# Turning two query blocks by DMA instead of on TensorE at the head of an attention and feed-forward kernel

## The chip, the cores and the metric

The kernel runs on one core of one Trainium2 chip. The core has a matrix engine (TensorE, PE in the profile, with its weight loads as PEld), a vector engine (VectorE, DVE), a scalar engine (ScalarE, ACT), a general engine (GpSimd, POOL) and a queue engine (SyncE, SP) that issues most transfers. Sixteen DMA engines move the data. Each engine works through its own list of instructions in order; semaphores make one wait for another. The metric is the device time of one execution in microseconds (us), as the median of the runs.

## The reference

Two blocks follow each other. The first is attention without softmax: for each batch and head, `kv = k^T v` and `out = q kv`, then an RMS norm over the 64 elements of a head. The second is a multiplicative feed-forward network over the 4608 tokens so made.

```python
kv = np.einsum('bhsd,bhse->bhde', k, v)
out = np.einsum('bhsd,bhde->bhse', q, kv)
rms = np.sqrt(np.mean(out * out, axis=-1, keepdims=True) + 1e-06)
x = (out / rms * g_norm)            # then (B,H,S,D) -> (B*S, H*D)
h = (x @ w1) * (x @ w2) @ w3
return h @ w_out
```

There are 8 batches, 8 heads, 576 tokens and a head size of 64; the model size is 512 and the inner size 1024. `q`, `k` and `v` are 32-bit floats; the weights arrive as 64-bit floats.

## The kernel before, in words

**Overall order.** Since nothing stands between the product with `w3` and the one with `w_out`, the kernel first multiplies `w3` by `w_out` (the fold). Then it walks over nine groups of 512 tokens: one for each batch, and one for the 64 tokens that each batch has left over. For each group it makes the two gate products with `w1` and `w2`, multiplies them, and projects with the folded matrix. The products use Winograd's scheme of seven block products instead of eight, so sums of blocks are made on VectorE. The attention of the next group runs in pieces between the products of the present one.

**Weights.** A 64-bit weight tile is read as raw words into one of four `raw` buffers and made into 32-bit floats by `conversion` (L137): two passes on ScalarE (L165, L167), then four on VectorE: the top bits of the low part (L169), a clamp (L173), a shift (L176) and an addition (L181). `w1` and `w2` are also scaled by the norm's gain (L135 or L133). `conversion` is a generator: each `yield` is a point at which the caller may place other work. With `in_parts`, which only one weight tile has, there is one more such point. `load_next` (L200, transfers at L207) fills the next raw buffer.

**The fold.** It goes over the inner size in eight chunks, twice (the first half of `w3`'s rows, then the second). For each chunk `w3` must be turned: `turn_w3` does it on TensorE (L701) and ScalarE copies the result out (L703); for chunks 3, 5 and 7 of the second half `w3_by_dma` does it by a DMA transpose. `fold_chunk` (L717) then adds a chunk to four sums; after the last chunk ScalarE copies each sum out (L723). `keep_warm` (L287) puts products of no use on TensorE.

**A turn by DMA** (`turn_by_dma`, L289). The DMA transpose works on 16-bit words. So the lower and upper halves of the 32-bit words are first split into two planes (L308 or L306), the transpose is issued on SyncE (L310), and the planes are put together again (L320). The split and the copy back are on GpSimd, ScalarE or VectorE, as the caller says. It too is a generator, with a point between each of its steps.

**The first batch.** Its attention runs inside the second half of the fold, in the loop that begins at L1470. `begin_q` (L1472) turns two of the four query blocks on TensorE (`q_t`, L361, transposes at L367, copy out at L369) and then loads the next blocks into the buffers that come free (`load_q_ahead`, L94): blocks 0 and 1 before chunk 1, blocks 2 and 3 before chunk 4. `begin_kv` makes `kv` (L347, copies at L355 and L357). `product` (L411) makes `q kv` for half of the heads (L425) after chunks 2 and 5, and `norm` follows: squares on ScalarE (L392), a reduction on VectorE (L393), the root on ScalarE (L397), the reciprocal (L399) and the multiplication (L402) on VectorE. The half of the first product is turned by DMA (`x_first`, L1474), the other half on TensorE (`turn`, L461, copy at L463). `sum_w` (L828, L829) and `combine_x` (L818) make the first sums of blocks for the gates. A `qT` tile holds a turned query block; there are two such buffers.

**The first gates.** `winograd` runs seven products (L748). After the first, ScalarE copies the result away (L766) before the third product may reuse its bank.

**What sets the order.** In the fold every engine's list is written out by hand, in the order in which the source runs. After it TensorE, GpSimd and SyncE keep that order, and a scheduler places the work of VectorE and ScalarE, except where `issue_after` ties a step behind a named instruction. One of those ties, at L1622, begins the conversion of a weight tile in the first gates. It is tied to `copies["xT"]`, the last copy of the turned second half:

```python
ahead = [copies["p5"][p] if p else copies["xT"], copies["u3" if p == 1 else "u2"][p]][n]
with tc.issue_after(ahead.ins):
```

Of the kernel before, what the change touches and what calls it, by code (L numbers as in the profile page):

```python
# [22 lines left out]
def kernel(  # L23
# [32 lines left out]
    nc = tc.nc  # L56
# [80 lines left out]
    def conversion(  # L137
        n, dst, raw, cols=slice(0, 1024), scale=None, by_scalar=False, in_parts=False
    ):

        dst, raw = (t if len(t.shape) == 3 else t[:, cols] for t in (dst, raw))
        if raw.dtype == FP32:
            yield
            yield
            if in_parts:
                yield
            nc.vector.tensor_copy(out=dst, in_=raw)
            if scale is not None:
                scale_by(dst, scale, by_scalar)
            return  # L150
        words = raw.bitcast(U32).rearrange("p (n w) -> p n w", w=2)
        lo, hi = words[:, :, 0], words[:, :, 1]

        low = ab[n % 2][:, NF // 2:].rearrange("p a i t -> p (a i t)")[:, cols]
        low_bits = low.bitcast(U32)

        low_top = low.bitcast(U16).rearrange("p (n w) -> p n w", w=2)[:, :, 1]
        hi_top = raw.bitcast(U16).rearrange("p (n w) -> p n w", w=4)[:, :, 3]
        if len(dst.shape) == 3:
            wide = dict(c=dst.shape[1])  # L160
            lo, hi, low, low_bits = (
                t.rearrange("p (c n) -> p c n", **wide) for t in (lo, hi, low, low_bits)
            )
        dst_bits = dst.bitcast(U32)
        nc.scalar.activation(low, lo, AF.Copy, scale=2.0 ** -51, bias=2.0)  # L165
        yield
        nc.scalar.activation(dst, hi.bitcast(FP32), AF.Abs)  # L167
        yield
        nc.vector.tensor_scalar(  # L169
            out=low_top, in0=hi_top, scalar1=0x8000, scalar2=0x4000,  # L170
            op0=ALU.bitwise_and, op1=ALU.bitwise_or,
        )
        nc.vector.tensor_scalar(  # L173
            out=dst, in0=dst, scalar1=LEAST, scalar2=MOST, op0=ALU.max, op1=ALU.min
        )
        nc.vector.tensor_scalar(  # L176
            out=dst_bits, in0=dst_bits, scalar1=3, scalar2=None, op0=ALU.logical_shift_left
        )
        if in_parts:
            yield  # L180
        nc.vector.tensor_tensor(out=dst_bits, in0=dst_bits, in1=low_bits, op=ALU.add)  # L181
        yield
        if scale is not None:
            scale_by(dst, scale, by_scalar)
# [145 lines left out]
    def attention(b):  # L330
# [37 lines left out]
            qT[r] = work.tile([P, 2, 2, P], FP32, name="qT")  # L368
            nc.scalar.copy(qT[r], qt_ps)  # L369

        def q_by_dma(r, copy=None):

            qT[r] = work.tile([P, 2, 2, P], FP32, name="qT")
            q_sb = loaded["q", b, r].rearrange("p e n -> p (e n)")
            to = qT[r].rearrange("p e i t -> p (e i t)")
            return turn_by_dma([q_sb], to, q_sb, [to], copy or q_copy)

        st = {}

# [333 lines left out]
    def fold_chunk(half, c, ms, cols=slice(0, DM)):  # L713
        if c == 0 and 0 in ms and cols.start == 0:
            sums_ps[half] = [bank(ps_mm, "mm") for m in range(NH)]
        for m in ms:
            nc.tensor.matmul(  # L717
                sums_ps[half][m][:, cols], lhsT=w3T[half, c][:, m, :], rhs=chunks[:, c, 1, cols],
                start=(c == 0 and cols.start == 0), stop=(c == KF - 1),
                skip_group_check=(half == 0),  # L720
            )
            if c == KF - 1:
                nc.scalar.copy(w3o_sb[:, half * NH + m, :], sums_ps[half][m])  # L723


    late = {}
# [688 lines left out]
    with tc.manual_schedule(  # L1415
# [22 lines left out]
        for c in range(KF):  # L1438
# [11 lines left out]
            if c == 0:  # L1450
                for n in range(2):
                    fold_chunk(0, c, range(NH), slice(n * N, (n + 1) * N))
                begin_next(lambda: turn_w3(0, 1))
                keep_warm(2)
                continue
            fold_chunk(0, c, range(NH - 1))
            if c < 3:
# [11 lines left out]
        turns, SPLIT = {}, {0: 3, 2: 5, 4: 7}  # L1469
        for c in range(KF):  # L1470
            if c in BEGIN:
                first.begin_q(2 * BEGIN[c], 2 * BEGIN[c] + 1)  # L1472
                if c == max(BEGIN):
                    x_first = first.x_by_dma(0, nc.vector.tensor_copy, split=nc.scalar.copy)  # L1474
                    next(x_first)
# [4 lines left out]
            if c < KF - 2:  # L1480
                if c < max(BEGIN):
                    begin_next()
                if c == max(BEGIN) + 1:
                    for steps_of_w in begun[len(converted)]:
                        next(steps_of_w)
                    all_of(x_first)
                else:
                    end_next(False)
# [3 lines left out]
                    next(t)  # L1492
                if len(raws) < FIRST:
                    load_next()
                if c == 2:
                    for steps_of_w in begun[len(converted)]:
                        next(steps_of_w)
                elif c == max(BEGIN):
                    run(sum_w(0))
            elif c == KF - 2:  # L1500
                end_next(False)
# [12 lines left out]
            fold_chunk(1, c, range(1, NH - 1))  # L1514
            if c == 2:
                all_of(turns[c + 1])
            elif c + 1 < KF and c + 1 not in turns:
                turn_w3(1, c + 1)
            if c in (max(BEGIN), KF - 2):
# [2 lines left out]
            if c in PRODUCT:  # L1522
                norms[c] = first.product(PRODUCT[c])
                next(norms[c])
                if c > max(BEGIN):
                    all_of(turns[c + 2])
                next(norms[c])
    fold_cm.__exit__(None, None, None)
    late_pool = ctx.enter_context(tc.tile_pool(name="late", bufs=1, reuse_waits="tile"))
# [6 lines left out]
    for n, T in enumerate(groups):  # L1536
# [44 lines left out]
        for p in range(NF):  # L1581
# [22 lines left out]
            if T == 0:  # L1604
# [14 lines left out]
                        run(ops)  # L1619
                for n in range(2):  # L1620
                    if len(converted) < len(todo):
                        ahead = [copies["p5"][p] if p else copies["xT"], copies["u3" if p == 1 else "u2"][p]][n]  # L1622
                        with tc.issue_after(ahead.ins):
                            if p or n:
                                begin_next()
# [83 lines left out]
```

## Time and profile before

| what | value |
|---|---|
| median of 3 runs | 741.33 us (739.96 to 741.8) |
| the profiled execution's own time | 740.67 us |
| its span, first to last instruction | 738.8 us |
| granted clock of TensorE, mean | 1.0 |
| TensorE busy | 733.8 us, 99% of the span |
| VectorE busy | 629.1 us, 85% |
| ScalarE busy | 378.9 us, 51% |
| GpSimd busy | 22.2 us, 3% |
| the second half of the fold | about 44.7 to 79.3 us |

Times in the profile are counted from the first instruction. A timeline line has start, duration, engine, source line, operation, tiles (out <- in), shapes, how many records were merged, and in brackets how long the engine was idle before and what released it. Two records of TensorE stand for one matmul in 32-bit floats. A line of the waits has the waiting engine and line, what it waited for, the total, the number of times and the longest. In the chain of waits each line is a piece of the chain of work that ended last: start, duration, what.

### The profile page before, as it was taken

Reading aid. Unit: us, or ns where it says so; the run is one execution under the profiler, and the core shown is the slowest. Engines: PE = TensorE matmul, PEld = TensorE weight load, DVE = VectorE, ACT = ScalarE, POOL = GpSimd, SP = SyncE. Lnnn points to the kernel's source line nnn. Section 1 sums busy time; section 2 is a strip of 40 time slices with the busy share of each in tenths; the row PEclk is TensorE's granted clock in tenths of the full one; section 3 lists DMA queues with packets and bytes.
Section 4 is the critical chain, followed back from the end, with each engine's and each line's share of the span. In section 5 each row is a group of like instructions: output and inputs, shape, how many; then the busy total and the mean of one; then the engine's idle time right before and its main releaser. Section 6 shows DMA issues by size and latency. Waiting matters only on the chain.

```text
span 738.8 us, 16924 instructions
## 1 busy us (share of the span) xinstructions
PE 733.8 (99%) x6867; PEld 659.5 (89%) x6867; DVE 629.1 (85%) x1259; ACT 378.9 (51%) x660; POOL 22.2 (3%) x29
## 2 busy tenths in 40 slices
PE   8999999999999999999999999999999999999998
PEld 7445788888899999999999999999999999999998
DVE  7988898968879689968996899689969987997797
ACT  7787778415552675257626762576177313212321
POOL 0000000221000000000000001000001000000000
PEclk9999999999999999999999999999999999999999
DMA  9999925599989698869887988698847762565454
GB/s 318 351 331 244 288 94 144 148 337 300 334 254 317 177 279 258 261 173 289 249 269 168 294 248 268 170 294 234 264 102 222 227 208 86 180 216 161 133 197 142
DMA packets 138769, 170.44 MB, mean 231 GB/s; under 512 B 81220, under 2 KB 114116, under 8 KB 138692
## 3 DMA queue, kind: packets, MB, share of 16 engines
q1 hardware_dynamic: 136240, 155.02, 70.8%
q10 hardware_dynamic: 2452, 14.35, 5.8%
q8 instruction: 54, 0.88, 0.5%
q14 instruction: 23, 0.19, 0.1%
HBM read 130.55 MB, written 20.71 MB: 205 GB/s over the span
## 4 chain that ended last, share of the span: by engine, by line
PE 94%; DMA 2%; ACT 2%; DVE 1%; SPq 1%; issue 0%; ACTq 0%
PE mm L748 37%; PE mm L1298 23%; PE mm L1040 21%; PE mm L717 5%; PE at L347 2%; DMA raw<-in_moe_w_dram 2%; PE at L748 2%; PE mm L425 1%; PE at L425 1%; PE at L701 1%; PE at L1341 0%; ACT ab L165 0%; SPq L207 0%; PE at L444 0%; ACT xT L306 0%
## 5 line engine op out<-in xcount | busy, mean ns | idle before, releaser
L1089 ACT COPY slots<-mm 128x512 f32<-128x512 f32 x88 | 51.6, 587 | 127.0 <-PE mm L1298 83.6
L748 PE MATMUL mm<-xT,w_sb 128*128 128x256 f32 x448 | 102.9, 380 | 0.0
L748 PEld LDWEIGHTS mm<-xT,w_sb 128*128 128x128 f32 x448 | 84.6, 191 | 11.3 <-issue 0.5
L748 PE MATMUL mm<-xc,ws 128*128 128x256 f32 x336 | 76.4, 380 | 0.3 <-ACT inner_sums L766 0.3
L748 PEld LDWEIGHTS mm<-xc,ws 128*128 128x128 f32 x336 | 63.9, 190 | 9.1 <-ACT inner_sums L766 0.7
L766 ACT COPY slots<-mm 128x512 f32<-128x512 f32 x59 | 34.6, 586 | 70.0 <-PE mm L748 65.0
L717 PE MATMUL mm<-chunks,ab 128*128 128x512 f32 (+1 forms) x136 | 59.7, 578 | 0.5 <-DVE chunks L181 0.5
L1093 DVE TENSOR_TENSOR slots<-mm,slots 128x512 f32<-128x512 f32 x66 | 45.2, 684 | 17.1 <-PE mm L1040 17.0
L1090 ACT COPY slots<-mm 128x384 f32<-128x384 f32 x88 | 42.3, 481 | 26.3 <-PE mm L1298 23.8
L1040 PE MATMUL mm<-ws,w3o_sb 128*128 128x128 f32 x350 | 54.0, 275 | 0.0
L1298 PE MATMUL mm<-w3o_sb,ab 128*128 128x128 f32 x368 | 48.9, 276 | 0.0
L393 DVE TENSOR_REDUCE inv<-sq 128x8 f32<-128x512 f32 (+1 forms) x40 | 24.6, 630 | 27.6 <-ACT sq L392 27.5
L1040 PEld LDWEIGHTS mm<-ws,w3o_sb 128*128 128x128 f32 x350 | 46.4, 192 | 0.0
L1298 PEld LDWEIGHTS mm<-w3o_sb,ab 128*128 128x128 f32 x368 | 45.4, 192 | 0.6
L717 PEld LDWEIGHTS mm<-chunks,ab 128*128 128x128 f32 x136 | 23.6, 190 | 22.6 <-issue 15.5
L1298 PE MATMUL mm<-w3o_sb,raw 128*128 128x128 f32 x340 | 43.5, 275 | 0.0
L1298 PEld LDWEIGHTS mm<-w3o_sb,raw 128*128 128x128 f32 x340 | 40.7, 192 | 0.0
L748 PE MATMUL mm<-xc,w_sb 128*128 128x256 f32 x160 | 38.5, 384 | 0.0
L1094 DVE TENSOR_TENSOR slots<-mm,slots 128x384 f32<-128x384 f32 x66 | 36.4, 552 | 2.2 <-PE mm L1298 1.6
L748 PE MATMUL mm<-xT,ws 128*128 128x256 f32 x160 | 38.2, 382 | 0.0
L748 PEld LDWEIGHTS mm<-xT,ws 128*128 128x128 f32 x160 | 30.1, 190 | 4.2 <-ACT slots L766 0.2
L748 PEld LDWEIGHTS mm<-xc,w_sb 128*128 128x128 f32 x160 | 29.9, 190 | 4.2
(246 smaller groups left out, 1648.9 us busy)
## 6 DMA issues: line engine op xcount, KB each, us to landing
w3o_sb<-w_l SPq DMA_DIRECT2D x21, 896.0 KB, 6.0
w3o_sb<-w3o_l SPq DMA_DIRECT2D x18, 896.0 KB, 6.4
raw<-in_moe_w_dram SPq DMA_DIRECT2D x31, 512.0 KB, 7.7
raw<-w3o_l SPq DMA_DIRECT2D x15, 896.0 KB, 4.7
w3o_sb<-w3o_l ACTq DMA_DIRECT2D x14, 896.0 KB, 4.6
k_sb<-in_k_dram SPq DMA_DIRECT2D x16, 576.0 KB, 5.0
v_sb<-in_v_dram SPq DMA_DIRECT2D x16, 576.0 KB, 5.9
q_sb<-in_q_dram SPq DMA_DIRECT2D x32, 256.0 KB, 4.8
```

The lines of the kernel that those rows point to most:

```text
L347: nc.tensor.matmul(ps[r * D:(r + 1) * D, :], lhsT=k_sb[rows, r, cols], rhs=v_sb[rows, r, cols], start=(j == 0), stop=(j == JS - 1),)
L393: adds["norm"] = nc.vector.tensor_reduce(out=inv[:, i], in_=sq.rearrange("p (h d) -> p h d", d=D), axis=AX.X, op=ALU.add)
L425: nc.tensor.matmul(o_ps[l][tokens, n * D:(n + 1) * D], lhsT=qT[r][rows, e, i, tokens], rhs=kv_b[rows, m // 2 ^ l, e, h, :], start=True, st ...
L717: nc.tensor.matmul(sums_ps[half][m][:, cols], lhsT=w3T[half, c][:, m, :], rhs=chunks[:, c, 1, cols], start=(c == 0 and cols.start == 0), s ...
L748: nc.tensor.matmul(ps[:, u, :], lhsT=lhsT(a_name, u, c), rhs=rhs(b_name, c),  start=(u == 0 and c == 0 and new), stop=(c == chunks - 1), s ...
L766: copies.setdefault(name, []).append(nc.scalar.copy(t, ps))
L1040: nc.tensor.matmul(ps[place // 4][:, place % 4, :], lhsT=x, rhs=y, start=new and place // 4 not in seen, stop=True, skip_group_check=True,)
L1089: nc.scalar.copy(z[:, 0:4], ps[0])
L1090: return nc.scalar.copy(z[:, 4:7], ps[1][:, 0:3])
L1093: nc.vector.tensor_add(z[:, 0:4], ps[0], z[:, 0:4])
L1094: nc.vector.tensor_add(z[:, 4:7], ps[1][:, 0:3], z[:, 4:7])
L1298: nc.tensor.matmul(ps[place // 4][:, place % 4, :], lhsT=x[:, c, :], rhs=y[:, c, :], start=new and place // 4 not in seen, stop=(c == 1), ...
```

## The change

Six edits, all before the end of the first gates:

- The third and fourth query block of the first batch (2 and 3) are turned by DMA transposes and no longer by `begin_q` on TensorE. Block 2 is split on ScalarE and block 3 on VectorE, after chunk 2's turn and ahead of the first norm; the two transposes are issued at chunk 3; at chunk 4 VectorE copies both back, ahead of `sum_w`.
- With that the loads of the next query blocks move on SyncE behind the transposes of `x_first` and of chunk 7.
- In the weight tile with `in_parts` there are now points after the first VectorE pass and after the clamp. The clamp runs between the second norm's reduction and its reciprocal, the shift and the addition behind the norm; before, clamp and shift ran ahead of the copies back of `x_first`.
- The extra point for weights that are already 32-bit floats goes; no tile of this case takes that branch.
- Four small products of no use are added before the second chunk of the fold.
- The first conversion of the gates is tied behind the last copy of the fold instead of the last `xT` copy.

```diff
 (conversion, 64-bit branch)
         nc.vector.tensor_scalar(out=low_top, in0=hi_top, ...)
+        if in_parts:
+            yield
         nc.vector.tensor_scalar(out=dst, in0=dst, scalar1=LEAST, scalar2=MOST, ...)
+        if in_parts:
+            yield
         nc.vector.tensor_scalar(out=dst_bits, in0=dst_bits, scalar1=3, ...)
-        if in_parts:
-            yield
         nc.vector.tensor_tensor(out=dst_bits, in0=dst_bits, in1=low_bits, op=ALU.add)
...
-        def q_by_dma(r, copy=None):
+        def q_by_dma(r, copy=None, split=None):
...
-            return turn_by_dma([q_sb], to, q_sb, [to], copy or q_copy)
+            return turn_by_dma([q_sb], to, q_sb, [to], copy or q_copy, split)
...
-                nc.scalar.copy(w3o_sb[:, half * NH + m, :], sums_ps[half][m])
+                copies["w3o"] = nc.scalar.copy(w3o_sb[:, half * NH + m, :], sums_ps[half][m])
...
                 begin_next(lambda: turn_w3(0, 1))
-                keep_warm(2)
+                keep_warm(2, 4)
...
             if c in BEGIN:
-                first.begin_q(2 * BEGIN[c], 2 * BEGIN[c] + 1)
+                if c == min(BEGIN):
+                    first.begin_q(0, 1)
...
                 if c == max(BEGIN) + 1:
-                    for steps_of_w in begun[len(converted)]:
-                        next(steps_of_w)
+                    steps_of_w, = begun[len(converted)]
+                    next(steps_of_w, None)
                     all_of(x_first)
...
+                if c == 3:
+                    for t in q_turns:
+                        next(t)
...
                 elif c == max(BEGIN):
+                    for r, t in enumerate(q_turns):
+                        all_of(t)
+                        first.load_q_ahead(2 + r)
                     run(sum_w(0))
...
             if c == 2:
                 all_of(turns[c + 1])
+                q_turns = [
+                    first.q_by_dma(2 + r, nc.vector.tensor_copy, split)
+                    for r, split in enumerate((nc.scalar.copy, nc.vector.tensor_copy))
+                ]
+                for t in q_turns:
+                    next(t)
...
                 next(norms[c])
                 if c > max(BEGIN):
                     all_of(turns[c + 2])
+                    next(steps_of_w, None)
                 next(norms[c])
...
-                        ahead = [copies["p5"][p] if p else copies["xT"], copies["u3" if p == 1 else "u2"][p]][n]
+                        ahead = [copies["p5"][p] if p else copies["w3o"], copies["u3" if p == 1 else "u2"][p]][n]
```

More of the change, by code (lines that the diff above doesn't have):

```diff
@@ L178, in conversion @@
         )
-        if in_parts:
-            yield
         nc.vector.tensor_tensor(out=dst_bits, in0=dst_bits, in1=low_bits, op=ALU.add)
```

## The prediction

> **What bounds the kernel now.** I read the busy shares first, then TensorE's own waits, then the stretch that the change touches in order of time, then the chain of waits past it.
>
> From the page:
>
> ```profile
> PE 733.8 (99%) x6867; PEld 659.5 (89%) x6867; DVE 629.1 (85%) x1259; ACT 378.9 (51%) x660; POOL 22.2 (3%) x29
> PEclk9999999999999999999999999999999999999999
> ```
>
> TensorE's waits, all of them:
>
> ```profile
> PE mm L287 <- POOL ident masks.py:199: 1.4, 1, 1.4
> PE mm L717 <- DVE chunks L181: 0.5, 1, 0.5
> PE mm L748 <- ACT inner_sums L766: 0.3, 1, 0.3
> ```
>
> TensorE is busy 733.8 of 738.8 us at the full granted clock. After its start it waits twice: 0.52 us for the fold's second chunk (13.32 to 13.84) and 0.26 us for a ScalarE copy (82.86 to 83.12). So a change at the kernel's beginning wins at most the TensorE work it removes plus these two waits, and any new TensorE wait there is paid in full, since nothing later is idle enough to give it back.
>
> The timeline around the removed transposes (start, duration, engine, line, idle time before in brackets):
>
> ```profile
> 55.33 1.16 PE L425 MATMUL at<-kv_sb,qT 64*64 64x64 f32 x64
> 56.54 1.08 ACT L392 ACTIVATE sq<-at 128x512 f32<-128x512 f32 x2 [1.74 <-PE at L425]
> 58.48 0.31 ACT L397 ACTIVATE inv<-inv,eps_col 128x16 f32<-128x16 f32 x1 [0.86 <-DVE inv L393]
> 58.70 1.13 ACT L165 ACTIVATE ab<-raw 128x1024 f32<-128x1024 uint32 x1
> 59.73 1.15 ACT L167 ACTIVATE chunks<-raw 128x1024 f32<-128x1024 f32 x1
> 60.40 1.04 PE L367 MATMUL at<-ident,q_sb 128*128 128x128 f32 x8
> 60.78 0.56 ACT L703 COPY ab<-at 128x512 f32<-128x512 f32 x1
> 61.40 1.13 PE L717 MATMUL mm<-chunks,ab 128*128 128x512 f32 x2
> ```
>
> The reader should see that ScalarE runs without a break from 58.48 to 61.34, and that the L717 at 61.40 (chunk 4 of the second half) starts 0.06 us after the L703 copy that makes its weights. The eight transposes fill time that TensorE would else wait.
>
> The chain of waits further on (start, duration, what):
>
> ```profile
> 72.27 8.51 DMA raw<-in_moe_w_dram
> 80.94 0.25 ACT ab L165
> 82.01 0.57 ACT w3o_sb L723
> 82.58 0.49 ACT inner_sums L766
> 83.12 14.08 PE mm L748 x64
> ```
>
> What the transfers moved (stretch, its length, ..., clock, DMA share, GB/s in the last column):
>
> ```profile
> 60.00:65.00 5.00, 5.00 (x87) 3.03 (x86) 4.84 (x7) 5.00 (x7) 0.00 (x0) 1.00 1.07 331
> 67.00:69.00 2.00, 2.00 (x6) 0.79 (x5) 1.82 (x4) 1.61 (x2) 0.00 (x0) 1.00 1.14 52
> ```
>
> In the chain a weight load lands at 80.78, its first ScalarE pass follows, then the fold's last copy, then the copy of the first product, which TensorE waits for.
>
> **The change part by part.**
>
> *TensorE's eight transposes go.* Their price is 0.87 us of issue (60.40 to 61.27), 1.00 us to the next L717. But that L717 waits for the L703 copy, which stands behind L397, L165 and L167 on ScalarE, all kept. It ended at 61.34, so without any other edit TensorE would still start at 61.40. Gain: 0, with 0.87 as the other end if that copy came 0.9 us sooner; nothing in the change moves it forward.
>
> *ScalarE's split of the third block is put ahead of the norm's squares.* It writes the buffer that the first product's first half reads, so it waits for that half: 55.33 + 0.58 + 0.05 = 55.96. Its load was issued at 46.48 and took 7.2 us, so it is there. The same operation takes 1.07 us at 77.43, 0.95 to the next start; I take 1.05, which gives the squares 57.01 in place of 56.54: +0.47. Behind them queue the reduction, the root, L165, L167 and the L703 copy, all back to back, so the copy ends at 61.81 and L717 starts at 61.87. TensorE idles from 60.40 to 61.87 and is 0.47 late from there on (bounds 0.37 and 0.6, from 0.95 and 1.07 and the half's place).
>
> *ScalarE loses two qT copies* (1.07 us at 61.25). So the two xT splits start at 61.81, not 62.20, and their transposes can be issued at 63.7, not 64.24. Worth 0 on the path: it serves only DMA work.
>
> *VectorE's split of the fourth block* (0.70, the same operation at 52.23) starts at 56.54 when the first product ends and is over at 57.2, before the squares' first result at 57.6: 0, in VectorE's idle 0.71. Without that idle time it would cost 0.7.
>
> *Two DMA transposes enter SyncE's queue* behind the raw load of 56.66; the two q loads of the next batch move behind the xT and chunk 7 transposes. Landings are in order of issue. The raw pair lands at 63.88 and 65.26, so the turned q follow 65.26. Two xT transposes landed 1.03 apart (69.19, 70.22), the first of them 2.66 behind the load ahead of it. I take 1.03 each, because in a full queue they are back to back: 66.3 and 67.3; upper ends 67.9 and 70.6. On SyncE itself an issue takes 1.24 to 1.31 us there (64.24, 65.52) and 4.21 behind a full queue (79.34); SyncE waited 3.1 us for L367 before, so issuing both costs 0 by the first and up to 5.8 us (2 x 2.9) for what is behind by the second. That is the same queue seen from its other end, and I don't add it. The q loads, moved by about 7 us, serve the ScalarE split at 77.43 that stands before the fold's last copies: landed at 65.87 before, they have 11.6 us to spare and need some 7 to 9; past 78 they would hold the gates' first copy, 1 us for each us.
>
> *Two VectorE copies back* (1.30, as the xT pair at 70.31). VectorE gets there at 65.05 + 0.47 = 65.52, so it waits: first 66.35, second 67.35 to 67.97. Then sum_w (65.05 to 67.71: 2.66), one L169 pass (0.64), the xT pair (1.30): 72.6. The squares of norm two, 0.47 late, allow the reduction at 72.21 + 0.47 = 72.68. So VectorE is just in time.
>
> *The weight passes spread.* The clamp (L173, 0.69) goes into the gap of the root (0.46 from 73.49 to 73.95): +0.23. The shift (0.73) goes behind the norm, into a stretch whose next consumer, TensorE's L748 at 80.97, had its operand at 78.12: hidden by 2.8 us. The norm ends at 75.60 + 0.47 + 0.23 = 76.30; TensorE's turn of it, at 75.80 + 0.47 = 76.27, waits about 0.1.
>
> *The tie behind the fold's last copy.* ScalarE's order L165, L723, L766 becomes L723, L165, L766. The L766 copy stays behind the weight pass that waits for the load; only the copy's 0.47 (82.01 to 82.48) leaves the line. Load to product was 83.12 - 80.78 = 2.34, and is now 1.87. Gain at most the 0.26 of TensorE's wait; loss 0, as the fold's copies are ready by 79.9 (79.25 and 0.57), before the load.
>
> *Four small matmuls* fit in the 0.52 us wait at 13.32: 44 records took 1.53 us at 7.06, so eight take below 0.3. Cost 0; 0.3 if that wait were gone. GpSimd's queue is unchanged, and past the gates' first product every engine's order is the old one.
>
> *The sum.* TensorE is ready for that product at 82.86 + 0.47 + 0.1 = 83.43. The load must then land by 83.43 - 1.87 = 81.56, 0.78 later than before. The added transposes take 2.06 us of queue, but from 67 to 69 us the engines moved 52 GB/s against 331 from 60 to 65, so most fits; I take 0.4 later, which is hidden. Against 83.12 that is +0.31 us. The profiled execution took 740.67 (span 738.8 and 1.9 around it), so 740.98; its median is 0.66 higher: 741.6.
>
> **Two rules beside the rows.** The row prices eight TensorE transposes at 0.87 us and a turn by DMA at 5.0 us from issue to landing (64.24), hidden if there is time. The Trainium skill, VectorE: DVE Perf Modes, § Rules for kernel authors, says to turn a 128x128 block on TensorE if PSUM will do, and by DMA otherwise; § The three transpose paths has 390 against 1309 ns. By that as an estimate, eight blocks would lose 7.4 us if nothing hid them; the sum above loses less as queue time is mostly free.
>
> A 256 KB q load lands 0.66 us behind the one before it, a transpose of equal size 1.03. The Trainium skill, Advanced Engine Details and Errata, § X-Bar Transpose (TRN2), calls transposes as fast as regular DMAs. By that the two would add 1.3 us of queue, not 2.06; the sum stays as it is.
>
> **The rivals.**
>
> *Late weights (slower).* Place: ScalarE's weight pass in front of the first product's copy. It decides once the load lands after 81.56, and costs 1 us for each us. For it: the queue holds the load for 8.5 us already, and moves 329 to 348 GB/s from 73 to 84. Against: the idle stretch from 65 to 71. Added transposes of 1.03 with nothing absorbed give 82.84, +1.6 in all: 742.9. Of 2.66 each: 86.1, +4.9: 746.2. Middle 744.2.
>
> *Late q (slower, less).* The third and fourth blocks land late and hold sum_w and the xT copies on VectorE, so the second norm. It starts with a landing after 67.4, 1 us each. One transpose at 2.66 lands the second at 68.95: +1.6, so +1.9 in all: 743.2. Its delay covers the first rival's, they don't add.
>
> *The gain shows.* TensorE wins 0.87 and 0.26: 740.2. This needs the L703 copy by 60.34, and ScalarE was full until 61.34.
>
> That the change doesn't do what it says is excluded by the order of the instructions: the eight transposes are gone from TensorE.
>
> **How the numbers follow.** The forecast 0.60 (its own range 741.0 to 742.3), late weights 0.20, late q 0.12, the gain 0.08. A measurement of this kernel tells about 0.3% (2.2 us) from no change: faster is below 739.1, slower above 743.55. The forecast and the gain are the same, but for 0.03 of scatter below; late weights are slower in 0.13, late q in 0.04. The range leaves out the upper half of late weights and takes in the gain: 740.3 to 744.0.
>
> **What would show it.** Right: no L367 beyond 46 us, TensorE idle about 1.5 us before an L717 near 61.9, released by L703; the squares near 57.0; the product of 83.12 within 83.2 to 83.7. Wrong: that L717 at 60.5 (the copy did not bind), a wait of over 1 us at L461 (late q), or L766 released after a load beyond 81.6 (late weights).

## The result, and the profile after

The changed kernel takes 743.38 us (742.97 to 744.45) against 740.74 us for the kernel before (739.96 to 741.8), a ratio of 1.0038 (95% interval 1.0027 to 1.0048): it is slower by 2.6 us. In a second comparison it took 743.89 us (742.00 to 748.25) against 740.38, ratio 1.0057 (1.0035 to 1.0079). (The ratio is estimated from the runs with its interval; it need not equal the quotient of the two medians.) The time lies inside the stated range of 740.3 to 744.0, but not where the forecast of 741.6 and its own range (741.0 to 742.3) had it: it lies in the part of the range that was there for the rival "late weights" (742.9 to 746.2). The profiled execution took 743.14 us.

The busy shares on the page after, and all waits of TensorE (waiting line, what it waited for, total, times, longest):

```profile
PE 732.5 (99%) x6867; PEld 657.5 (89%) x6867; DVE 629.9 (85%) x1262; ACT 378.6 (51%) x659; POOL 22.2 (3%) x29
```

```profile
PE mm L748 <- ACT inner_sums L766: 1.9, 1, 1.9
PE mm L287 <- POOL ident masks.py:199: 1.4, 1, 1.4
PE mm L717 <- ACT ab L703: 1.3, 1, 1.3
PE at L701 <- DVE chunks L181: 0.8, 1, 0.8
```

TensorE does 1.28 us less (732.47 against 733.75, unrounded), and waits more. In place of 0.52 for a chunk at 13.3 us there is 0.76 for a chunk at 6.0 us; in place of 0.26 for the first gate product's copy there is 1.90; and 1.35 for the L703 copy is new. Together: -1.28 + 0.24 + 1.64 + 1.35 = 1.95 us, and the last TensorE group, L1341, starts 1.96 us later (734.16 against 732.20). The 1.28 is not all the change's: 0.87 are the transposes that are gone, 0.30 come back as the small products, and 0.72 are the first 22 products of no use, which took 4.34 us in this profile and 5.06 in the one before (4.18 to 5.06 over all fourteen profiles). So by place it is -0.18 at the start, +0.48 at 60 us and +1.64 at 83 us.

The starts of the same TensorE groups in both timelines show where this arises:

| TensorE group | before | after | later by |
|---|---|---|---|
| first product, L425 | 55.33 | 55.18 | -0.15 |
| fold of chunk 4, L717, second part | 61.40 | 61.76 | 0.36 |
| second product, L425 | 70.31 | 70.67 | 0.36 |
| turn of the second norm, L461 | 75.80 | 76.16 | 0.36 |
| third product of the first gates, L748 | 83.12 | 85.13 | 2.01 |
| last group, L1341 | 732.20 | 734.16 | 1.96 |

So there are two places: 0.5 us at 60 us, and 1.65 us at 83 us. Everything from there on keeps its distance. First place, timeline after:

```profile
55.99 1.05 ACT L308 COPY qT<-q_sb 128x1024 uint16<-128x1024 uint16 x1 [1.34 <-PE at L425]
56.94 1.08 ACT L392 ACTIVATE sq<-at 128x512 f32<-128x512 f32 x2
61.15 0.56 ACT L703 COPY ab<-at 128x512 f32<-128x512 f32 x1
61.76 1.13 PE L717 MATMUL mm<-chunks,ab 128*128 128x512 f32 x2 [1.35 <-ACT ab L703]
```

The eight transposes that filled this time are gone, and the copy that TensorE needs comes 0.37 us later than before (it ends at 61.71 against 61.34). Second place, the chain of waits after (start, duration, what):

```profile
73.73 0.94 SPq L207
74.67 0.04 issue
74.71 8.64 DMA raw<-in_moe_w_dram
...
84.51 0.57 ACT inner_sums L766
85.08 0.04 issue
85.13 14.08 PE mm L748 x64
```

The weight load was issued at 72.27 before and flew 8.51 us; now it is issued at 74.71 and flies 8.64. It lands at 83.36, 2.58 us later. The tie gives 0.57 of that back, since landing to product takes 1.77 in place of 2.34: 2.01. So it is the issue that is late. SyncE's timeline, before and then after (start, duration of the issue, line, operation):

```profile
56.66 1.13 SPq L207 DMA_DIRECT2D raw<-in_moe_w_dram  x2
61.03 0.88 SPq L94 DMA_DIRECT2D q_sb<-in_q_dram  x2
64.24 2.60 SPq L310 DMA_TRANSPOSE xn<-xT  x2
66.94 2.47 SPq L310 DMA_TRANSPOSE chunks<-ab  x1
69.94 0.38 SPq L104 DMA_DIRECT2D k_sb<-in_k_dram  x1
```

```profile
56.66 1.13 SPq L207 DMA_DIRECT2D raw<-in_moe_w_dram  x2
57.88 7.46 SPq L310 DMA_TRANSPOSE q_sb<-qT  x2
65.46 2.58 SPq L310 DMA_TRANSPOSE xn<-xT  x2
68.15 2.11 SPq L310 DMA_TRANSPOSE chunks<-ab  x1
70.81 0.89 SPq L94 DMA_DIRECT2D q_sb<-in_q_dram  x2
71.79 0.65 SPq L104 DMA_DIRECT2D k_sb<-in_k_dram  x1
```

The two added transposes hold SyncE for 7.46 us (4.41 and 2.96), until 65.33. The xT transposes behind them are issued 1.22 later, though ScalarE splits their data earlier than before; the end of chunk 7's issue is 0.85 later; the two query loads, now in front of `k`, put 1.0 more between; longer issues of `k` and the first weight load bring the rest of the 2.44.

How full the DMA engines were (after; ..., clock, DMA share, GB/s last), in the two stretches that the prediction showed:

```profile
60.00:65.00 5.00, 3.65 (x78) 1.93 (x78) 4.84 (x8) 4.99 (x8) 0.00 (x0) 1.00 1.12 235
67.00:69.00 2.00, 2.00 (x6) 0.90 (x5) 1.82 (x4) 0.96 (x1) 0.00 (x0) 1.00 1.02 230
```

The share adds up the times that packets took, so it can pass 1. The stretch from 67 to 69 us, which moved 52 GB/s before, was not idle: its DMA share was 1.14 then, as the prediction's own line shows, and the transposes of `x_first` and of chunk 7 were in flight. In the profile after, 69 to 71 us looks the same: 74 GB/s at a share of 1.29, behind the transposes that now come later. How much more would have fitted there is not shown.

### The profile page after: what moved, and what is told of

Its sections match the earlier page's. It is cut to its first block, busy times and chain, and to the rows that moved or that the text cites. A ratio compares the mean times of both kernels' runs of the same rounds, so it can differ in the third digit from the quotient of the medians.

```text
span 741.0 us, 16935 instructions
## 1 busy us (share of the span) xinstructions
PE 732.5 (99%) x6867; PEld 657.5 (89%) x6867; DVE 629.9 (85%) x1262; ACT 378.6 (51%) x659; POOL 22.2 (3%) x29
## 4 chain that ended last, share of the span: by engine, by line
PE 96%; DMA 2%; ACT 1%; DVE 1%; SPq 0%; issue 0%; ACTq 0%
PE mm L748 37%; PE mm L1298 23%; PE mm L1040 21%; PE mm L717 6%; PE at L347 3%; PE at L748 2%; DMA raw<-in_moe_w_dram 2%; PE mm L425 1%; PE at L425 1%; PE at L701 1%; PE at L1341 0%; PE at L444 0%; PE mm L287 0%; ACT ab L163 0%; DVE inv L393 0%
## 5 line engine op out<-in xcount | busy, mean ns | idle before, releaser
L748 PE MATMUL mm<-xT,w_sb 128*128 128x256 f32 x448 | 102.9, 379 | 0.0
L748 PEld LDWEIGHTS mm<-xT,w_sb 128*128 128x128 f32 x448 | 84.4, 190 | 11.5 <-issue 0.5
L748 PE MATMUL mm<-xc,ws 128*128 128x256 f32 x336 | 76.4, 379 | 1.9 <-ACT inner_sums L766 1.9
L748 PEld LDWEIGHTS mm<-xc,ws 128*128 128x128 f32 x336 | 63.8, 190 | 10.9 <-ACT inner_sums L766 2.3
L766 ACT COPY slots<-mm 128x512 f32<-128x512 f32 x59 | 34.5, 585 | 69.8 <-PE mm L748 64.8
L717 PE MATMUL mm<-chunks,ab 128*128 128x512 f32 (+1 forms) x136 | 59.8, 577 | 1.4 <-ACT ab L703 1.3
L1298 PE MATMUL mm<-w3o_sb,ab 128*128 128x128 f32 x368 | 48.9, 276 | 0.0
L1298 PEld LDWEIGHTS mm<-w3o_sb,ab 128*128 128x128 f32 x368 | 45.4, 192 | 0.6
L717 PEld LDWEIGHTS mm<-chunks,ab 128*128 128x128 f32 x136 | 23.6, 190 | 24.1 <-issue 15.8
L1298 PE MATMUL mm<-w3o_sb,raw 128*128 128x128 f32 x340 | 43.5, 275 | 0.0
L1298 PEld LDWEIGHTS mm<-w3o_sb,raw 128*128 128x128 f32 x340 | 40.7, 192 | 0.0
L748 PE MATMUL mm<-xc,w_sb 128*128 128x256 f32 x160 | 38.5, 384 | 0.0
L748 PE MATMUL mm<-xT,ws 128*128 128x256 f32 x160 | 38.1, 381 | 0.0
L748 PEld LDWEIGHTS mm<-xT,ws 128*128 128x128 f32 x160 | 30.1, 190 | 4.3 <-ACT slots L766 0.2
L748 PEld LDWEIGHTS mm<-xc,w_sb 128*128 128x128 f32 x160 | 29.8, 190 | 4.2
```

Source lines behind the costliest of these rows:

```text
L717: nc.tensor.matmul(sums_ps[half][m][:, cols], lhsT=w3T[half, c][:, m, :], rhs=chunks[:, c, 1, cols], start=(c == 0 and cols.start == 0), s ...
L748: nc.tensor.matmul(ps[:, u, :], lhsT=lhsT(a_name, u, c), rhs=rhs(b_name, c),  start=(u == 0 and c == 0 and new), stop=(c == chunks - 1), s ...
L766: copies.setdefault(name, []).append(nc.scalar.copy(t, ps))
L1298: nc.tensor.matmul(ps[place // 4][:, place % 4, :], lhsT=x[:, c, :], rhs=y[:, c, :], start=new and place // 4 not in seen, stop=(c == 1), ...
```

## The experiments

The theory: the query transposes and the moved loads delay the weight load through SyncE's queue, which costs the time at 83 us, and the L703 copy keeps TensorE from using the time that its transposes left. Rivals: the other edits cost it; the L703 wait is the loss and the load only follows; only bytes in the queue count. Profiles of different runs differ at the start (TensorE's waits before 14.1 us add up to between 0.4 and 1.4 us), so waits and flights are compared first, and absolute times only with care. The flight of the deciding load scatters too, by more than a microsecond (below), and each version has one profile. In one table (load: the one that the first product's copy stands behind; waits of TensorE at L717 for L703, at L461, and behind L766 copies):

| version | median | ratio to before (95%) | load issued, lands | waits |
|---|---|---|---|---|
| before | 740.4 to 740.7 | | 72.27, 80.78 | 0, 0, 0.26 |
| changed | 743.38 | 1.0038 (1.0027 to 1.0048) | 74.71, 83.36 | 1.35, 0, 1.90 |
| changed, again | 743.89 | 1.0057 (1.0035 to 1.0079) | 75.68, 85.36 | 1.35, 0, 3.13 |
| query part undone | 741.13 | 1.0007 (0.9998 to 1.0016) | 72.32, 79.40 | 0, 0, 0 |
| query part alone | 744.52 | 1.0052 (1.0040 to 1.0064) | 74.79, 83.24 | 1.35, 0.27, 1.40 |
| weights first | 741.52 | 1.0016 (1.0007 to 1.0025) | 72.36, 79.69 | 1.34, 0, 0 |
| tied behind the product | 743.21 | 1.0040 (1.0028 to 1.0053) | 74.26, 83.91 | 1.36, 0, 1.81 |
| loads moved only | 741.34 | 1.0013 (1.0004 to 1.0022) | 74.10, 81.49 | 0, 0, 0.56 |
| plain loads for transposes | 742.12 | 1.0026 (1.0015 to 1.0037) | 74.01, 82.42 | 0, 0, 1.40 |
| one block by DMA | 741.28 | 1.0011 (1.0003 to 1.0020) | 72.34, 79.86 | 0.41, 0, 0 |
| weights first, copy early | 741.30 | 1.0013 (1.0005 to 1.0022) | 71.99, 79.01 | 0, 0.62, 0 |
| and norm first | 740.28 | 0.9998 (0.9990 to 1.0007) | 72.27, 79.60 | 0, 0, 0 |
| and one block | 740.41 | 1.0001 (0.9992 to 1.0009) | 70.08, 75.36 | 0, 0, 0 |
| norm first, no small products | 740.08 | 0.9992 (0.9983 to 1.0001) | 72.31, 77.58 | 0, 0, 0 |

Not in the table: in the profiles of "loads moved only" and "one block by DMA" TensorE also waits 0.96 and 0.57 us near 229 us, at L1298, for a later load. No other of these profiles has such a wait. It is part of those two profiled times and may be part of their medians; its cause was not tested.

### Which part: the query part undone, and alone

Undone in the changed kernel (the lines that turn blocks 2 and 3 by DMA go out):

```diff
             if c in BEGIN:
-                if c == min(BEGIN):
-                    first.begin_q(0, 1)
+                first.begin_q(2 * BEGIN[c], 2 * BEGIN[c] + 1)
...
```

> The third and fourth query block are turned on TensorE again, with their loads in the old place; the spread passes, the tie and the four small matmuls stay. Theory (the loss comes through SyncE's queue and the weight load): the load lands near 80.8 again, the first gates' product starts within 0.3 us of 82.9, and the time is 740.3 to 740.9, ratio to before 0.9995 to 1.0002. Rival A (the spread passes or the tie cost the time): it stays at 742.5 or more. So the query part alone should carry the whole 2.6 us.

Measured: 741.13, 0.2 above the expected stretch and with no difference to the kernel before that can be told; no wait for a product's copy, landing 79.40. The landing came 1.4 us sooner than in the profile before, from the same time of issue, so flights scatter by that much.

Alone: the kernel before with only those lines.

> The kernel before with the query part alone: third and fourth block turned by DMA, the old place of the weight passes, the old tie, no added small matmuls. Theory: the loss of the change is all here, and the old tie leaves the fold's last copy between the late load and the product (2.34 us from landing to product in place of 1.77): 743.4 to 744.2, ratio 1.004 to 1.005; TensorE waits 1.3 us for L703 and 2.0 to 2.6 us for the product's copy. Rival D (the other parts cost a part of the loss): 742.7 or less.

Measured: 744.52, above the expected stretch. Landing to product took 2.27 us (83.24 to 85.51), near the 2.34 of the old tie; the wait is shorter than expected because TensorE was ready for the product 0.88 us later than in the changed kernel (84.11 against 83.23), in part by a wait of 0.27 at L461. The whole loss is in the query part: undone, it goes; alone, it is all there. Rivals A and D fall. The tie's 0.5 us is read from the two profiles; the times (744.52 against 743.38 and 743.89) fit it but do not show it by themselves.

### Is it the load: the weights first, and the tie

Weights first, in the changed kernel:

```diff
-                first.begin_kv(BEGIN[c])
-                if c == max(BEGIN):
-                    load_q_left(1)
+                if c == max(BEGIN):
+                    first.kv(1)
+                else:
+                    first.begin_kv(BEGIN[c])
...
-                for _ in range(3):
-                    load_next()
+                for _ in range(1):
+                    load_next()
+                load_four("kv", 1, 0)
+                load_q_left(1)
+                for _ in range(2):
+                    load_next()
```

> The changed kernel with one thing moved on SyncE: the loads of k, v and the left-over queries for the second batch are issued behind the first pair of weight loads, not ahead of it. All engines keep their order. Theory: the weight load is issued near 72.2 to 72.8 in place of 74.71 and has 1.3 MB less ahead of it, so it lands by 79.5; TensorE's wait of 1.90 us for the product's copy goes, down to 0.2 at most, and the time falls by 1.6 to 1.9 us, to 741.5 to 741.8 (ratio 1.001 to 1.0016); the wait of 1.35 us before the L717 stays. Rival B (TensorE's new wait for the L703 copy is the loss, and the load only fills it): no more than 0.4 us comes back, 743 or more. k and v are first read at 99 us, so their delay of some 2 us should cost nothing.

Measured: 741.52, as the theory had it. TensorE's waits in this profile:

```profile
PE mm L287 <- POOL ident masks.py:199: 1.4, 1, 1.4
PE at L701 <- DVE chunks L181: 1.3, 1, 1.3
PE mm L717 <- ACT ab L703: 1.3, 1, 1.3
```

The wait behind L766 is gone though the transposes, the moved loads and every engine's order are still there; only three loads that nobody needs before 97 us went behind two. This shows the late load as the cause of about 1.9 us (743.38 against 741.52; the two intervals of the ratio, 1.0027 to 1.0048 and 1.0007 to 1.0025, do not touch), and rival B falls. It also rules out VectorE as the cause. The profile before names VectorE's pass on `ab` (L169, in the changed kernel L167) as what ScalarE's weight pass waited for, since it ended 0.01 us after the load landed, and in the profile after it starts 1.2 us later (81.23 against 80.04). But here ScalarE's pass starts at 80.81 and VectorE's only at 81.69, so the one does not wait for the other.

The tie:

```diff
-ahead = [copies["p5"][p] if p else copies["w3o"], ...
+ahead = [copies["p5"][p] if p else copies["p1"][0], ...
```

> The changed kernel with the first gates' weight conversion tied behind the copy of their first product in place of the fold's last copy: ScalarE does the L766 copy and then the L163 pass that waits for the load. Theory: the product of 85.13 starts near 83.3, so 1.8 us come back there; but the next L766 copy now stands behind both weight passes (load 83.36, two passes of 1.05, copy 0.5: 86.1), so the product after it, ready at 85.1, waits about 1.0. Net 0.8 us less: 742.4 to 742.8 (ratio 1.0023 to 1.0028). If the weight pass in front of the copy is not what holds TensorE, nothing comes back: 743.4.

Measured: 743.21, above the expected stretch and no gain that can be told. The wait did move from the third product to the fourth, but it was 1.81 us, not 1.0:

```profile
81.53 0.59 ACT L766 COPY inner_sums<-mm 128x512 f32<-128x512 f32 x1 [1.19 <-PE mm L748]
84.01 1.15 ACT L163 ACTIVATE ab<-raw 128x1024 f32<-128x1024 uint32 x1 [1.89 <-DMA raw<-in_moe_w_dram]
85.06 1.11 ACT L165 ACTIVATE w_sb<-raw 128x1024 f32<-128x1024 f32 x1
86.07 1.06 ACT L766 COPY slots<-mm 128x512 f32<-128x512 f32 x2
```

The first copy no longer waits, and the second stands behind both passes. The load flew 9.65 us and landed 0.55 later than in the changed kernel, and TensorE, not held up, was ready earlier. How much of the missing 0.8 us is this flight and how much the other order is not shown; at the measured median the new tie did not pay.

### What makes the load late: moved loads, bytes, transposes

Both blocks on TensorE, the two query loads left in their new place:

```diff
                 if c == min(BEGIN):
                     first.begin_q(0, 1)
+                else:
+                    for r in (2, 3):
+                        first.q_t(r)
...
-                    for r, t in enumerate(q_turns):
-                        all_of(t)
+                    for r in range(2):
                         first.load_q_ahead(2 + r)
...
```

> The third and fourth query block are turned on TensorE, but the two query loads of the next batch stay where the change puts them, behind the xT and chunk 7 transposes; so SyncE issues what it issued before, with these two in another place. Theory: the moved loads alone put 0.98 us of issue and 0.5 MB (some 1.3 us of queue) ahead of the weight load: it lands at 81.7 to 82.2, the product starts at 83.4 to 84.0, the time is 741.2 to 741.8. The remaining 1.6 to 2.2 us of the change's loss then belong to the two transposes. Rival C (the queue has room and only the transposes' issue time counts): load within 0.3 us of 80.8, time 740.3 to 740.9.

Measured: 741.34, landing 81.49, wait 0.56. In this profile the moved loads alone use up the slack of the load and a little more. Rival C does not hold in it: the load lands 0.7 us after 80.8, and its issue is 1.8 us later than before (74.10 against 72.27). By time alone this version cannot be told from the one with the query part undone (741.13).

The same with two plain loads in the transposes' place:

```diff
+                if c == 3:
+                    for r in range(2):
+                        nc.sync.dma_start(
+                            out=w3o_sb[:, KF - 2 + r, :].rearrange("p (h n) -> p h n", h=2),
+                            in_=q[0, 4 + 2 * r:6 + 2 * r, 0:G, :].rearrange("h (p j) d -> p h (j d)", j=J),
+                        )
```

> The version with both query blocks turned on TensorE and the two query loads moved behind the seventh chunk (741.3 us, profiled load landing at 81.49), with two plain loads of 256 KB each added at the place in SyncE's queue where the change issues its two DMA transposes; they go to memory that is written later, and nothing reads them. Theory (a DMA transpose holds SyncE and the DMA engines longer than its bytes do): plain loads take 0.5 us of issue each and 0.66 us of queue, SyncE is free again by 59.5, before the xT splits end near 63.7, so the weight load is at most 0.6 us later than without them: 741.2 to 742.0, against 743.4 to 743.9 with the transposes. Rival G (any 0.5 MB more in that place delays the load as much): 743 or more, with a wait of 1.5 us or more for the product's copy.

Measured: 742.12, just outside the expected stretch; landing 0.93 us later than without them, not 0.6, and a wait of 1.40. So neither the theory nor rival G (743 or more) had it fully. SyncE in this version:

```profile
57.95 3.68 SPq L1501 DMA_DIRECT2D w3o_sb<-in_q_dram  x2
64.15 4.13 SPq L310 DMA_TRANSPOSE xn<-xT  x2
68.40 1.24 SPq L310 DMA_TRANSPOSE chunks<-ab  x1
69.75 1.43 SPq L94 DMA_DIRECT2D q_sb<-in_q_dram  x2
```

The deciding load is issued as early as without the plain loads (74.01 against 74.10) and flies 1.02 us longer (8.42 against 7.40). That may be their bytes in the queue, but it is less than the 1.4 us by which flights scatter, so it is not shown. With transposes the load is issued 0.70 later still (74.71) and flies 0.22 longer. By time the three versions stand in this order, 741.34, 742.12 and 743.38, but the intervals of neighbours overlap, so the split between moved loads, bytes and transposes is read from single profiles. The issue is the firmer half: in the four profiles with both blocks turned by DMA and the loads in the change's order it comes at 74.26 to 75.68, in the two with the query part as before at 72.27 and 72.32. The transposes' data is not slower: they land at 66.35 and 67.26, the plain loads at 66.36 and 68.58. What differs is SyncE, held for 7.46 us against 3.68: until 65.33, past the time at which the xT splits are ready (63.60), where the plain loads are issued by 61.63 and the xT transposes start at 64.15, as in the kernel before (64.24). The Trainium skill, Advanced Engine Details and Errata, § X-Bar Transpose (TRN2), calls transposes as fast as regular DMAs; these landings agree, and what the transposes cost more here lay in the issue. Issuing them from another engine's queue, which would take that time off SyncE, was not tried.

Only the fourth block by DMA, split on VectorE:

```diff
-                q_turns = [
-                    first.q_by_dma(2 + r, nc.vector.tensor_copy, split)
-                    for r, split in enumerate((nc.scalar.copy, nc.vector.tensor_copy))
-                ]
-                for t in q_turns:
-                    next(t)
+                q_turns = [first.q_by_dma(3, nc.vector.tensor_copy, nc.vector.tensor_copy)]
+                next(q_turns[0])
...
```

> The changed kernel with the third query block turned on TensorE again and only the fourth by DMA (its split on VectorE; its next load stays behind the seventh chunk). Theory: SyncE is through with one transpose at 62.3, before the xT splits are over near 63.7, so the xT and chunk transposes start as early as before, and only the one moved load (0.5 us) stays in front: the weight load is issued at 72.5 to 73.5 and lands at 80.3 to 82.0, the time is 740.3 to 741.5, less than a third of the change's loss; the squares are not held up, so TensorE waits 0.5 us at most before L717. Rival H (the loss goes by halves with the blocks): 741.8 to 742.3.

Measured: 741.28, landing 79.86, no wait behind L766 and 0.41 before L717. SyncE issues the one transpose from 57.52 to 61.90 and the xT transposes at 63.87, as early as before. So the loss does not go by halves (741.8 to 742.3 lies mostly outside the interval, 740.6 to 741.9): the load's part of it is gone once SyncE is free when the next transposes are ready. One moved load fewer stands in front as well, so this version does not separate the two.

### The other wait, and what stands behind it

Weights first, and the turn of chunk 4 with its L703 copy ahead of the two weight passes:

```diff
-                if c < max(BEGIN):
+                if c == 3:
+                    begin_next(lambda: turn_w3(1, 4), 0)
+                elif c < max(BEGIN):
                     begin_next()
...
-            elif c + 1 < KF and c + 1 not in turns:
+            elif c != 3 and c + 1 < KF and c + 1 not in turns:
                 turn_w3(1, c + 1)
```

> The changed kernel with the first weight pair ahead of the k, v and left-over query loads on SyncE, and the third chunk's TensorE turn and its L703 copy put ahead of the two weight passes on ScalarE. Theory: the wait of 1.34 us before L717 goes; but the second norm on VectorE runs behind the landings of the turned queries (66.4 and 67.4 us) and of the xT pair (71.4 us) and had only 0.34 us of idle time ahead of its reduction, so TensorE waits about 1.0 us at L461 (turn of the normed block) instead. Time 741.0 to 741.4, at most 0.4 us under the version with only the weights first. Rival E (nothing else stands behind that wait): no wait at L461, 740.0 to 740.3.

Measured: 741.30. The wait before L717 is gone, and TensorE waits at L461 instead, in two pieces, 0.62 in all where about 1.0 was expected:

```profile
75.22 0.33 PE L461 MATMUL at<-ident,xn 128*128 128x128 f32 x1 [0.35 <-DVE xn L402]
75.82 0.98 PE L461 MATMUL at<-ident,xn 128*128 128x128 f32 x7 [0.27 <-DVE xn L402]
```

In this profile VectorE waits 0.58 and 0.17 us for the turned queries, and the xT copies start at 71.12, after the landing at 71.03. So the place of the prediction's rival "late q" shows here, once the two waits before it are gone. The timed gain over "weights first" is too small to tell.

VectorE's order changed on top of that:

```diff
+                    run(sum_w(0))
                     for r, t in enumerate(q_turns):
                         all_of(t)
                         first.load_q_ahead(2 + r)
-                    run(sum_w(0))
...
-                    all_of(x_first)
+                    all_of(x_first[0])
...
                 if c > max(BEGIN):
-                    all_of(turns[c + 2])
-                    next(steps_of_w, None)
+                    all_of(x_first[1])
                 next(norms[c])
+                if c > max(BEGIN):
+                    all_of(turns[c + 2])
```

with `x_first` as two separate turns, and the clamp's step behind the norm.

> As the last, and VectorE's work re-ordered so that the norm can follow the earlier product: the sums of the weights ahead of the query copies back (they fill the wait for the landing), one of the two xT copies behind the norm's reductions, the clamp behind the norm, and on ScalarE the root ahead of the seventh chunk's copy back. Theory: TensorE waits 0.4 us at most in all at the second product and at L461; TensorE's work is the removed transposes shorter with no wait in their place, so 740.0 to 740.6, ratio 0.999 to 1.000, 0.9 to 1.4 us under the version with only the weights first. Rival F (the DMA work that came in slows other transfers, so that a new load is late): TensorE waits over 0.5 us at a line not named here and the time stays at 741 or more.

Measured: 740.28, and TensorE waits nowhere after the start:

```profile
PE mm L287 <- POOL ident masks.py:199: 1.4, 1, 1.4
PE at L701 <- DVE chunks L181: 1.1, 1, 1.1
```

The whole loss is back, 3 us against the changed kernel, with both blocks still turned by DMA, and rival F falls. But the time is that of the kernel before. One reason shows in the runs: the span is 0.4 us shorter (median 738.1 against 738.5 beside it), but the time outside it is 2.10 to 2.22 us in every run of this version and 1.79 to 1.91 in every run of the kernel before beside it, which takes 0.3 of it back. With one block by DMA and the same order:

> Only the fourth block turned by DMA, with the re-ordering of the version that had no waits left (first weight pair ahead of k and v, third chunk's turn and copy ahead of the weight passes, weight sums ahead of the query copy, norm ahead of the second xT copy and of the clamp). Theory: TensorE does 0.45 us less than before and waits at none of the named places; 739.7 to 740.4, ratio 0.999 to 1.000, the same as with both blocks within what can be told. Rival I (half the DMA work leaves room that the version with both blocks lacked, in places that its waits do not show): below 739.6, faster than before by over 0.1%.

Measured: 740.41, and rival I falls. And the version with both blocks without the four small products (`keep_warm(2)`):

> The version with both blocks turned by DMA and no wait left past the start, without the four small matmuls that the change adds near 13.3 us. In its profile TensorE's wait at the start came at 6.1 us (1.09 us), not at 13.3, so the small matmuls had no wait to lie in and cost up to 0.30 us (0.91 us for twelve warming matmuls against 0.61 for the first ones alone). Theory: 739.9 to 740.3, ratio to before 0.9992 to 0.9998. Rival J (they shorten another wait of the start by what they cost): no change, 740.3 or more, with a wait of 0.2 to 0.5 us before the L717 near 13.5 us in its place.

Measured: 740.08, ratio 0.9992 (0.9983 to 1.0001): not shown faster. A wait of 0.27 us came back before the L717 at 13.9, as rival J had it, while the time lies where the theory put it; the 0.2 us between this version and the one above cannot be told from nothing. No version is shown to beat the kernel before.

### The changed kernel again

> The changed kernel itself, to stand beside the others of this comparison: 743.0 to 743.8, waits of 1.3 to 1.4 us before L717 and of 1.6 to 2.2 us before the third product of the first gates.

Measured: 743.89, runs from 742.00 to 748.25, where the kernel before stayed between 740.02 and 740.76 beside it. Its profile is of a run of 746.88, with the load landing at 85.36 after a flight of 9.68 and a wait of 3.13; its mean granted clock of 0.997 against 1.0 accounts, as an estimate (0.003 times 741), for some 2 us of the rest. The run of 748.25 shows 0.995; the other four, at 1.0, took 742.00 to 744.10. So the wide spread is in part the clock and in part the load's flight.

## Why the prediction was wrong, step by step

The measured time fell into the range of 740.3 to 744.0, but the account behind the 741.6 did not hold, so the number was met by luck: the range had been widened to take in the lower half of "late weights", which had a chance of 0.20. That rival named the right place (ScalarE's weight pass in front of the first product's copy) and the right price (1 us for each us of lateness past 81.56). Its reason, 2.06 us more of queue for the load to fly through, is not what the profile shows: the flight grew by 0.13 and the issue came 2.44 later.

**TensorE's transposes gain nothing: right.** L717 was forecast at 61.87 behind the L703 copy and started at 61.76, released by it, after 1.35 us of waiting (1.47 forecast). With that copy early the wait was gone.

**The ScalarE split costs 0.47: right.** Squares at 56.94 (57.01 forecast), copy over at 61.71 (61.81).

**Landings of the turned queries, VectorE's chain: right.** 66.35 and 67.26 (66.3 and 67.3), the xT copies over at 72.73 (72.6), L461 at 76.16 with no wait (76.27 with 0.1). The q loads' slack held: they landed at 74.72 for a split at 77.80.

**The tie: right.** 1.77 us from landing to product (1.87 forecast), and 2.27 with the old tie.

**Four small products cost 0: not settled.** The wait that was to cover them came at 6.0 us, not at 13.3, in the profile after. The version without them ran 0.2 us shorter, within the uncertainty.

**The load lands "0.4 later, which is hidden": wrong, and this is the step that failed.** It landed 2.58 later, and only 0.78 was free. Of the 2.58, 2.44 are the issue on SyncE, a term that the sum put at nothing. Two arguments led to it. The first was that the issue time of the transposes "is the same queue seen from its other end, and I don't add it". It is not the same: in these timelines SyncE issues one thing after the other, so 7.46 us of issuing held the xT transposes to 65.46 when their data was ready at 63.6, and everything behind them. The prediction had the row and even a price of up to 5.8 us for what stands behind, which it did not add: two issues at its 4.21 us, from 57.88 on, end at 66.3, which is 2.6 past the 63.7 that it gave for the xT data. This comparison was left out. The second was that "most fits" because the engines moved only 52 GB/s from 67 to 69 us. The share in the same line was 1.14, so the row does not support it; but in the profile after the flight is only 0.13 longer, so this argument is not what made the load late. The two moved loads were counted for the slack of their own data, but not as 1.0 us of issue in front of the weight load.

**Time around the span taken as constant: off by 0.3.** The forecast used 1.9 us around the span. Wherever a run's span is on record, it is 1.8 to 1.9 in the four kernels that turn blocks 2 and 3 on TensorE (before, undone, loads moved, plain loads) and 2.1 to 2.2 in those that turn one or both by DMA. What it is was not tested.

**The sum.** Product at 85.13 in place of 83.43: 1.70. The span's end after the last TensorE work and the time around it add the rest of the 2.16 us between 740.98 and the profiled 743.14. The forecast's 741.6 also stood on a median of 741.33 for the kernel before, from three runs; over six it is 740.74. So a rise of 0.3 us was forecast and one of 2.6 measured.

**Small slips.** By its own rows (61.81 and 2.01) the xT splits end at 63.8, not 63.7, and the middle between 742.9 and 746.2 is 744.5, not 744.2. The estimate of 7.4 us takes 390 and 1309 ns from the Trainium skill, VectorE: DVE Perf Modes, § The three transpose paths, which gives them for 16-bit blocks; the blocks here have 32-bit words, so it does not carry over. Nothing in the sum rests on these.

## What to carry to other kernels

Price an added DMA by following every issue behind it on its queue to the engine that waits for it, with the issue time and not only the flight; and compare its end with the time at which the next issue's data is ready. A low rate in bytes per second was no sign of idle DMA engines here (52 GB/s at a share of 1.14): read the busy share in the same line. Work taken off a busy engine is worth what the next dependency allows. Here a ScalarE copy, a queue order and a VectorE order had to be changed before the loss was gone, and even then no version was shown to be faster than the kernel before.

## What was not expected of the hardware

Issuing one DMA transpose of 256 KB took SyncE 4.41 and 2.96 us behind two loads in flight (4.38 and 2.75 in another run, 3.02 and 3.29 in the version without the small products), against 1.23 to 1.31 for the xT transposes right after; two plain loads of that size in the same place took 2.04 and 1.59. The same weight load, issued at 72.27 and 72.32 behind the same transfers, flew 8.51 us in one run and 7.08 in another. And kernels with blocks turned by DMA spent 0.3 us more outside the profiled span; its cause is open.
